# Attention, mixture of experts and feed-forward in one kernel: transposes moved a step, loads by head pair, weights placed earlier

## The chip, the cores and the metric
The kernel runs on one core of a Trainium2 chip. The metric is device time in microseconds (us) of one execution of the whole program; lower is better. Each version is run several times and the median counts.

The engines are named as in the profile: PE is TensorE (matmuls), PEld its weight loads, DVE is VectorE, ACT is ScalarE, POOL is GpSimd, and SP is the queue engine that issues most DMAs.

## The reference
The program computes three layers one after the other. B = 4 batches, H = 12 heads, S = 448 positions, D = 64; N = B*S = 1792 tokens with DM = 768 values; E = 8 experts with FF = 1024; the last layer has F2 = 2048.

```
scores = q @ k.T / sqrt(D) - log(S);  attn = sigmoid(scores);  x = attn @ v     # x: (N, DM)
logits = x @ w_gate;  e = argmax(logits);  g = softmax(logits)[e]
y = g * (relu(x @ w1[e]) @ w2[e])                                               # one expert per token
h = y @ w_in;  out = (h * sigmoid(h)) @ w_out
```

All operands are fp32, except that w_in and w_out arrive as 64-bit words that the kernel decodes.

## The kernel before
Every operand of the accurate matmuls is split into a high part rounded to fp32r and a low part, the difference; a product is three matmuls (high by high, low by high, high by low). The program's order on each engine is written out by hand: an engine runs its instructions in the order in which the code issues them, and waits where an operand isn't there. All DMAs but the gathers and scatters go through SP's queue, which is also in order.

Attention. A head pair (two heads) is handled in four half-steps k, each with 128 of the keys; there are 24 pairs, so k runs to G = 96 in a loop with step 2 (L616). One pass of the loop issues `scores(k)` and `scores(k+1)` (L212: score matmuls on half the rows of PE for each head, the sigmoid on ACT), then `av` of two half-steps earlier (L228: value matmuls in plain fp32), then DVE's splits of the next unit (two pairs, L180 to L204), then `evac` (L240: ACT copies a finished pair's output from PSUM), and then `background` (L604), which takes one `xform` from the list `xq`. `xform` (L246) is half a pair: two matmuls against the identity and the gate's weights (L258) transpose the output to token rows and give its part of the logits; DVE copies the rows (L260) and adds the logits (L265), and every second pair SP stores the rows to Xd (L268). After the last pair of a batch `route` (L270) works out experts, ranks and gate values in small DVE operations, some per half-step, and stores the gates to Gd (L365, rows of one value). After the third batch `choose` (L368) finds the expert with most tokens so far and SP loads its first-layer weights to stage1 (L390); in the last 12 half-steps they are split in half rows (L640 to L646, the subtractions half on DVE and half on POOL).

`load` (L167) fetches q, k and v of a unit of two pairs; two units are in flight.

Tiles of experts. Tile 0 belongs to the chosen expert. After the loop SP loads that expert's second-layer weights to stage2 (L746), `xtrans` (L673) transposes tile 0, the last `xform` and route run, `tables` (L418) lays out the other tiles in some 50 DVE operations, and `split2` (L692) splits stage2 on ACT, DVE and POOL. A tile (L802) is `l1` (L698), `relu`, `htrans` (L710), `l2` (L720) and `yout` (L736), which scales by the gate gathered from Gd (`gate`, L546). At an expert's last tile the next weights are split and loaded. The first expert's successor gets its stage2 in two parts during and after tile 1 (L827, L853).

Between the tiles `early` (L577) decodes six slices of w_in and w_out, one at a time; five are stored for later, one to the SBUF tile `sqp` and four to DRAM (Wd, L585), and `keep0` (L590) splits the sixth. The feed-forward layer begins with reloads from Wd on SP and POOL (L955), gathers of token rows (`xload`, L783), their transposes (L889, two PSUM buffers), and splits of the reloaded slices on ACT and DVE (`wlater`, L960). Then 112 steps of 18 plus 12 matmuls follow.

Of the kernel before, what the change touches and what calls it, by code (L numbers as in the profile page):

```python
# [26 lines left out]
E, FF = 8, 1024  # L27
# [30 lines left out]
def attn_moe_ffn(ctx: ExitStack, tc, qT, kT, v, wg, w1, w2, w_in, w_out, out):  # L58
# [19 lines left out]
    Wd = dp.tile([GROUPS[0], 128, 2, DM], F32, name="Wd")  # L78
# [46 lines left out]
    sqp = RX.pool("w10", 1).tile([128, DM], F32, name="w10")  # L125
# [14 lines left out]
    vp_ = LA.pool("a_v", 3)  # L140
    ld = LA.pool("a_load", 2)
# [9 lines left out]
    zero = c2.tile([128, YW], F32, name="zero")  # L151
    nc.vector.memset(zero, 0.0)
    xf = c2.tile([128, NP, 128 + E], F32, tag="xf", name="xf")
# [13 lines left out]
    def load(un, parts=(slice(0, 2),)):  # L167
        b, u = units[un]
        kf = ld.tile([128, 2, KP], F32, tag="kf", name=f"kf{un}")
        qf = ld.tile([128, 2, S], F32, tag="qf", name=f"qf{un}")  # L170
        vf = vp_.tile([128, 2, 4, 128], F32, tag="vf", name=f"vf{un}")
        for i, p in enumerate(parts):
            hs = slice(2 * u + p.start, 2 * u + p.stop)
            nc.sync.dma_start(out=kf[:, p], in_=kT[b, hs].rearrange("r p s -> p r s"))
            nc.sync.dma_start(out=qf[:, p], in_=qT[b, hs].rearrange("r p s -> p r s"))
            if i == 0:
                nc.sync.dma_start(out=vf, in_=v[b, :, 2 * u:2 * u + 2])
        loads[un] = kf, qf, vf

    def split_tiles(un):  # L180
        t = lambda n, w: sp_.tile([128, 2, w], F32R, tag=n, name=f"{n}{un}")
        ops[un] = t("kh", KP), t("kl", KP), t("qh", S), t("ql", S)

    def cast_k(un, p=slice(0, 2)):
        nc.vector.tensor_copy(out=ops[un][0][:, p], in_=loads[un][0][:, p])

    def sub_k(un, p=slice(0, 2)):
        kh, kl = ops[un][:2]
        nc.vector.tensor_sub(out=kl[:, p], in0=loads[un][0][:, p], in1=kh[:, p])

    def cast_q(un, p=slice(0, 2), copy=nc.vector.tensor_copy):
        copy(out=ops[un][2][:, p], in_=loads[un][1][:, p])

    def sub_q(un, p=slice(0, 2)):
        qh, ql = ops[un][2:]
        nc.vector.tensor_sub(out=ql[:, p], in0=loads[un][1][:, p], in1=qh[:, p])

    def first(p):
        cast_q(0, p, nc.scalar.copy)
        cast_k(0, p)  # L200
        sub_k(0, p)
        sub_q(0, p)

    SPLITS = (cast_k, cast_q, sub_k, sub_q)  # L204
# [7 lines left out]
    def scores(k):  # L212
        pr, g = divmod(k, NG)
        un, p = divmod(pr, 2)
        kh, kl, qh, ql = (t[:, p] for t in ops[un])
# [12 lines left out]
    def av(k):  # L228
        pr, g = divmod(k, NG)
        un, p = divmod(pr, 2)  # L230
        vf = loads[un][2]
        if g == 0:
            po[pr] = ps_o.tile([128, 512], F32, tag="o", name=f"o{pr}")
        a, n = gt.pop(k)
        for i in range(2):
            r = slice(64 * i, 64 * i + 64)
            nc.tensor.matmul(out=po[pr][r, 0:S], lhsT=vf[:, p, g, r], rhs=a[:, i if n == 2 else 0],  # L237
                             start=(g == 0), stop=(g == NG - 1))
# [31 lines left out]
    def route(b):  # L270
# [33 lines left out]
        nc.scalar.activation(out=sp, in_=z, func=AF.Sigmoid, bias=zero[:CP, 0:1])  # L304
        nc.scalar.activation(out=sn, in_=z, func=AF.Sigmoid, bias=zero[:CP, 0:1], scale=-1.0)
# [59 lines left out]
        nc.sync.dma_start(out=Gd[b * S:(b + 1) * S].rearrange("(c p) f -> p c f", p=CP), in_=gs.unsqueeze(2))  # L365
        yield "gs"

    def choose():  # L368
        yield 0
        pn = px_[1][:, 448:448 + E]  # L370
        nc.tensor.matmul(out=pn, lhsT=ones, rhs=run, start=True, stop=True)
        yield 0
        mx = rt.tile([128, 1], F32, tag="cmx", name="cmx")
        nc.vector.tensor_reduce(out=mx, in_=pn, axis=AX.X, op=ALU.max)
        yield 1
        cd = rt.tile([128, E], F32, tag="ccd", name="ccd")
# [12 lines left out]
        for i in range(KC):  # L389
            nc.sync.dma_start(out=stage1[:, i], in_=w1[bass.ds(er, 1), :, i].rearrange("a p f -> (a p) f"))  # L390
        yield 1
# [161 lines left out]
    load(0, (slice(0, 1), slice(1, 2)))  # L553
    load(1)
    split_tiles(0)
    first(slice(0, 1))
# [13 lines left out]
    PRE = [*range(1, 2 * GROUPS[0]), 0]  # L570
# [6 lines left out]
    def early():  # L577
        i = len(done)
        bt = c2.tile([128, DM], I32, tag="xf", name=f"btp{i}")
        sq = c2.tile([128, DM], F32, tag="sq", name=f"sqp{i}")  # L580
        for _ in decode(raws.pop(), sq, bt):
            pass
        f, o = divmod(PRE[i], 2)
        if PRE[i]:
            nc.sync.dma_start(out=sqp if (f, o) == (1, 0) else Wd[f, :, o], in_=sq)  # L585
# [4 lines left out]
    def keep0():  # L590
        wi = xr_p[1].tile([128, 2, DM], F32R, tag="xr", name="wi0")
        nc.scalar.copy(out=wi[:, 0], in_=done[-1])
        nc.vector.tensor_sub(out=wi[:, 1], in0=done[-1], in1=wi[:, 0])
# [10 lines left out]
    def background(k):  # L604
        for x in list(tasks):
            advance(x, RATE[x in fast])
        if xq and (k % 2 == 1 or k >= G - 4):
# [3 lines left out]
            if u == NU - 1 and pr % 2 == 1 and half == 1:  # L611
# [4 lines left out]
    for k in range(0, G + LAG + 2, 2):  # L616
        un, r = divmod(k, UG)
        if k < G:
            if r == (0 if un else 4) and un + 2 < len(units):
                load(un + 2)  # L620
            scores(k)
            scores(k + 1)
        if LAG <= k < G + LAG:
            av(k - LAG)
            av(k - LAG + 1)
        o = r - 2 * (un == 0)
        if k < G and un + 1 < len(units) and 0 <= o < len(SPLITS):
            if o == 0:
                split_tiles(un + 1)
            SPLITS[o](un + 1)  # L630
            SPLITS[o + 1](un + 1)
        if k == 0:
            first(slice(1, 2))
        if k >= LAG and (k - LAG) % NG == NG - 2:
            pr = (k - LAG) // NG
            evac(pr)
            xq += [(pr, 0), (pr, 1)]
        for j in (k, k + 1):
            background(j)
            if G - UG <= j < G - UG + 2 * KC:  # L640
                i, o = divmod(j - (G - UG), 2)
                hs = slice(o * HB, o * HB + HB)
                cast = nc.scalar.copy if i >= 4 else nc.vector.tensor_copy
                eng = nc.gpsimd if o else nc.vector
                cast(out=w1h[:, i, hs], in_=stage1[:, i, hs])
                eng.tensor_sub(out=w1l[:, i, hs], in0=stage1[:, i, hs], in1=w1h[:, i, hs])  # L646
# [12 lines left out]
    stage2 = wp2.tile([128, FC, DM], F32, name="stage2")  # L659
# [84 lines left out]
    er = reg(es_i[0:1, 0:1], (SP,), E - 1)  # L744
    for f in range(FC):
        nc.sync.dma_start(out=stage2[:, f], in_=w2[bass.ds(er, 1), :, f].rearrange("a p f -> (a p) f"))  # L746
    xhl = xtrans(0, cur[0])
    for x in xq:
        xform(*x)
# [52 lines left out]
    for t in range(TMAX):  # L802
# [6 lines left out]
        if t > 0:  # L809
# [16 lines left out]
            if t == 1:  # L826
                nc.sync.dma_start(out=stage2[:, 0:SA], in_=wsrc(w2, ne1, 0, SA))  # L827
            if len(done) == len(PRE) and not wi0:
# [23 lines left out]
        if t == 1:  # L852
            nc.sync.dma_start(out=stage2[:, SA:], in_=wsrc(w2, ne1, SA, FC))  # L853
# [8 lines left out]
    R0.close()  # L862
    M1.close()
# [79 lines left out]
    src = {(0, 1): dc.tile([128, DM], F32, tag="sq0", name="sqw")}  # L943
    for f in range(1, GROUPS[0]):
        w = wtile(0, f)
        wt[0, f] = w[:, 0], w[:, 1]
        r = dc.tile([128, 2, DM], F32, tag=f"raw{f % 2}", name=f"wd{f}")
        src[f, 0], src[f, 1] = sqp if f == 1 else r[:, 0], r[:, 1]
    later = sorted(src, key=lambda x: (x[0] + FLAG * x[1], x[1]))
    for i, (f, o) in enumerate(later):  # L950
        if i == 2:
            xts1 = xload(1)
        if i:
            eng = nc.sync if i < 2 else nc.gpsimd
            eng.dma_start(out=src[f, o], in_=Wd[f, :, o])  # L955
# [148 lines left out]
```

## Time and profile before

| | us |
|---|---|
| median of 3 runs | 1097.03 (1094.67 to 1097.07) |
| profiled execution | 1096.06 |
| its span | 1094.0 |
| PE busy | 1032.5 |
| DVE busy | 580.5 |
| ACT busy | 424.6 |
| POOL busy | 115.5 |

The span is the time between the first and the last record of the execution; what lies outside it belongs to start and end. The profile places attention at 0 to about 206 us, the tiles up to about 588 us, and the feed-forward layer behind that. "PEclk" and "granted clock" are the share of full speed at which PE ran (1.00 is 2.4 GHz, 0.50 is 1.2 GHz). A wait is written as the waiting instruction, an arrow, and the instruction that released it.

### The profile page before, as it was taken

How to read it: one execution, taken by the hardware profiler on the slowest of the kernel's cores; microseconds unless marked ns; L12 is line 12 of the kernel's file. 1: busy time of each engine (PE TensorE's matmuls, PEld its weight loads, DVE VectorE, ACT ScalarE, POOL GpSimd, SP SyncE). 2: the span in 40 equal slices, each digit the busy share in tenths (PEclk: the TensorE clock that was granted, in tenths of full speed). 3: DMA queues.
4: the chain of work that ended last, by engine and by line, in shares of the span. 5: the costliest groups of instructions: out<-in, count | busy, mean ns of one | idle time of the engine just before them, and what ended most of it. 6: DMA issues, size and time to landing. Idle time of an engine off the chain costs nothing. (4 is left out here: it accounts for less than half of the span.)

```text
span 1094.0 us, 16957 instructions
## 1 busy us (share of the span) xinstructions
PE 1032.5 (94%) x6418; PEld 901.3 (82%) x6418; DVE 580.5 (53%) x1167; ACT 424.6 (39%) x714; POOL 115.5 (11%) x106
## 2 busy tenths in 40 slices
PE   7999999888999999999997899999999999999996
PEld 4444444567987888888886899999999999999996
DVE  4234355583599218571712566476477455557443
ACT  5454444432487227462612455333233222223110
POOL 1000000331122202121112110000000000000022
PEclk9999999989999999999999899999999999999998
DMA  6444646449599317772624765564445544455572
GB/s 222 125 126 127 166 122 163 117 147 278 172 365 344 143 44 269 279 253 95 216 103 143 274 222 198 190 241 151 174 173 186 204 160 144 173 202 206 198 289 117
DMA packets 49150, 205.75 MB, mean 188 GB/s; under 512 B 7968, under 2 KB 16416, under 8 KB 45088
## 3 DMA queue, kind: packets, MB, share of 16 engines
q1 hardware_dynamic: 44288, 184.09, 48.5%
q0 software_dynamic: 4768, 20.47, 5.4%
q8 instruction: 52, 0.85, 0.3%
q14 instruction: 42, 0.34, 0.1%
HBM read 170.30 MB, written 33.84 MB: 187 GB/s over the span
## 5 line engine op out<-in xcount | busy, mean ns | idle before, releaser
L993 ACT ACTIVATE sg<-fh 128x256 f32<-128x256 f32 x112 | 42.9, 383 | 230.1 <-PE fh L991 218.1
L991 PE MATMUL fh<-rxh,w 128*128 128x256 f32 x462 | 130.5, 282 | 0.0
L990 PE MATMUL fh<-rxl,w 128*128 128x256 f32 x462 | 130.4, 282 | 0.0
L989 PE MATMUL fh<-rxh,w 128*128 128x256 f32 x462 | 130.2, 282 | 0.0
L1026 PE MATMUL fy<-w,gh 128*128 128x384 f32 x364 | 122.5, 337 | 0.4 <-DVE acc L1039 0.4
L1027 PE MATMUL fy<-w,gh 128*128 128x384 f32 x364 | 121.9, 335 | 0.0
L1028 PE MATMUL fy<-w,gl 128*128 128x384 f32 x364 | 121.8, 335 | 0.0
L224 ACT ACTIVATE a<-s,bias 128x896 f32<-128x896 f32 x96 | 82.7, 910 | 94.9 <-PE s L221 94.7
L994 DVE TENSOR_TENSOR sg<-sg,fh 128x256 f32<-128x256 f32 x112 | 47.0, 420 | 132.2 <-ACT sg L993 132.2
L728 PE MATMUL y<-w2h,hl 128*128 128x384 f32 x304 | 103.8, 342 | 10.2 <-DVE hl L717 7.0
L726 PE MATMUL y<-w2h,hh 128*128 128x384 f32 x304 | 106.3, 350 | 0.7 <-ACT hh L716 0.7
L727 PE MATMUL y<-w2l,hh 128*128 128x384 f32 x304 | 103.2, 339 | 0.5 <-POOL w2l L696 0.4
L703 PE MATMUL h<-w1h,xl 128*128 128x512 f32 x228 | 90.5, 397 | 2.9 <-DVE xl L684 2.9
L701 PE MATMUL h<-w1h,xh 128*128 128x512 f32 x228 | 92.3, 405 | 0.9 <-ACT xh L683 0.9
L702 PE MATMUL h<-w1l,xh 128*128 128x512 f32 x228 | 90.2, 396 | 0.0
L991 PEld LDWEIGHTS fh<-rxh,w 128*128 128x128 f32 x462 | 88.1, 191 | 0.0
L990 PEld LDWEIGHTS fh<-rxl,w 128*128 128x128 f32 x462 | 87.8, 190 | 0.0
L989 PEld LDWEIGHTS fh<-rxh,w 128*128 128x128 f32 x462 | 87.7, 190 | 0.0
L717 DVE TENSOR_TENSOR hl<-x,hh 128x512 fp32r<-128x512 f32 x38 | 26.2, 688 | 113.0 <-ACT hh L716 108.7
L237 PE MATMUL o<-a,vf 128*64 128x448 f32 x384 | 82.5, 552 | 0.0
L260 DVE COPY xr<-x 112x256 f32<-112x256 f32 x48 | 20.3, 424 | 106.6 <-PE x L258 106.6
L998 DVE TENSOR_TENSOR gl<-sg,gh 128x256 fp32r<-128x256 f32 x112 | 47.8, 426 | 52.9 <-ACT gh L997 51.5
(220 smaller groups left out, 2202.0 us busy)
## 6 DMA issues: line engine op xcount, KB each, us to landing
rxh<-Td SPq DMA_DIRECT2D x35, 768.0 KB
rxl<-Td SPq DMA_DIRECT2D x35, 768.0 KB
stage<-w SPq DMA_DIRECT2D x14, 1536.0 KB
stage<-w SPq DMA_DIRECT2D x8, 1920.0 KB
raw<-w_in SPq DMA_DIRECT2D x13, 768.0 KB
raw<-w_out SPq DMA_DIRECT2D x13, 768.0 KB
stage<-w SPq DMA_DIRECT2D x8, 1152.0 KB
Yd<-ys SPq DMA_DIRECT2D x19, 384.5 KB
```

The source lines that it names most:

```text
L701: nc.tensor.matmul(out=ph, lhsT=xh[:, k], rhs=w1h[:, k, cs], start=(k == 0), stop=False)
L702: nc.tensor.matmul(out=ph, lhsT=xh[:, k], rhs=w1l[:, k, cs], start=False, stop=False)
L703: nc.tensor.matmul(out=ph, lhsT=xl[:, k], rhs=w1h[:, k, cs], start=False, stop=(k == KC - 1))
L726: nc.tensor.matmul(out=o, lhsT=hh[:, c], rhs=w2h[:, f, ys], start=(f == 0), stop=False)
L727: nc.tensor.matmul(out=o, lhsT=hh[:, c], rhs=w2l[:, f, ys], start=False, stop=False)
L728: nc.tensor.matmul(out=o, lhsT=hl[:, c], rhs=w2h[:, f, ys], start=False, stop=(f == FC - 1))
L989: nc.tensor.matmul(out=ph, lhsT=ih[:, k], rhs=xh[:, k], start=(k == 0), stop=False)
L990: nc.tensor.matmul(out=ph, lhsT=ih[:, k], rhs=xl[:, k], start=False, stop=False)
L991: nc.tensor.matmul(out=ph, lhsT=il[:, k], rhs=xh[:, k], start=False, stop=(k == KC - 1))
L1026: nc.tensor.matmul(out=o, lhsT=gh[:, c], rhs=w[1][:, 0, ys], start=(f == 0), stop=False)
L1027: nc.tensor.matmul(out=o, lhsT=gh[:, c], rhs=w[1][:, 1, ys], start=False, stop=False)
L1028: nc.tensor.matmul(out=o, lhsT=gl[:, c], rhs=w[1][:, 0, ys], start=False, stop=last)
```

## The change
The transposing matmuls of a pair are issued in the pass after its `evac`, all of the pair's together, between that pass's scores and values; `background` no longer issues them. Loads and splits go by single pairs (q first), loads three pairs ahead. After `choose`, SP also loads the chosen expert's second-layer weights to stage2, which has its own place; the load after the loop is gone. The splits of stage1 go by whole rows, casts in turn on DVE and ACT, subtractions on DVE. Gd is stored from ACT's queue. `sqp` has four places: five of the six decoded slices stay there, one is stored to Wd and reloaded; the order of slices changes, and `keep0` runs as soon as two are decoded. The first part of the successor's stage2 load moves from the middle to the end of tile 1. The last route is no longer begun twice.

```diff
-    Wd = dp.tile([GROUPS[0], 128, 2, DM], F32, name="Wd")
+    Wd = dp.tile([128, DM], F32, name="Wd")
...
-    sqp = RX.pool("w10", 1).tile([128, DM], F32, name="w10")
+    sqp = RX.pool("w10", 1).tile([128, 4, DM], F32, name="w10")
+    RS = Group("right")
+    stage2 = RS.pool("stage2", 1).tile([128, FC, DM], F32, name="stage2")
...
-    vp_ = LA.pool("a_v", 3)
-    ld = LA.pool("a_load", 2)
+    vp_ = LA.pool("a_v", 5)
+    ld = LA.pool("a_load", 3)
...
+    def load(pr):
+        b, p6 = divmod(pr, NP)
+        kf = ld.tile([128, KP], F32, tag="kf", name=f"kf{pr}")
+        qf = ld.tile([128, S], F32, tag="qf", name=f"qf{pr}")
+        vf = vp_.tile([128, 4, 128], F32, tag="vf", name=f"vf{pr}")
+        nc.sync.dma_start(out=qf, in_=qT[b, p6])
+        nc.sync.dma_start(out=kf, in_=kT[b, p6])
+        nc.sync.dma_start(out=vf, in_=v[b, :, p6])
+        loads[pr] = kf, qf, vf
...
+    def split_k(pr):
+        kh, kl = ops[pr][:2]
+        nc.vector.tensor_copy(out=kh, in_=src(pr, 0))
+        nc.vector.tensor_sub(out=kl, in0=src(pr, 0), in1=kh)
+
+    def split_q(pr, copy=nc.vector.tensor_copy):
+        qh, ql = ops[pr][2:]
+        copy(out=qh, in_=src(pr, 1))
+        nc.vector.tensor_sub(out=ql, in0=src(pr, 1), in1=qh)
...
-        nc.sync.dma_start(out=Gd[b * S:(b + 1) * S].rearrange("(c p) f -> p c f", p=CP), in_=gs.unsqueeze(2))
+        nc.scalar.dma_start(out=Gd[b * S:(b + 1) * S].rearrange("(c p) f -> p c f", p=CP), in_=gs.unsqueeze(2))
...
             nc.sync.dma_start(out=stage1[:, i], in_=w1[bass.ds(er, 1), :, i].rearrange("a p f -> (a p) f"))
+        for f in range(FC):
+            nc.sync.dma_start(out=stage2[:, f], in_=w2[bass.ds(er, 1), :, f].rearrange("a p f -> (a p) f"))
...
-    load(0, (slice(0, 1), slice(1, 2)))
-    load(1)
+    for pr in range(3):
+        load(pr)
     split_tiles(0)
-    first(slice(0, 1))
+    split_q(0, nc.scalar.copy)
+    split_k(0)
...
-    PRE = [*range(1, 2 * GROUPS[0]), 0]
+    PRE = [2 * GROUPS[0] - 1, *range(2 * GROUPS[0] - 1)]
+    SLOT = [3, 3, 0, 1, 2, 3]
...
-        sq = c2.tile([128, DM], F32, tag="sq", name=f"sqp{i}")
+        sq = sqp[:, SLOT[i]]
...
-        f, o = divmod(PRE[i], 2)
-        if PRE[i]:
-            nc.sync.dma_start(out=sqp if (f, o) == (1, 0) else Wd[f, :, o], in_=sq)
+        if i == 0:
+            nc.sync.dma_start(out=Wd, in_=sq)
...
-        if xq and (k % 2 == 1 or k >= G - 4):
+
+    def wsplit0(i):
+        (nc.scalar.copy if i % 2 else nc.vector.tensor_copy)(out=w1h[:, i], in_=stage1[:, i])
+        nc.vector.tensor_sub(out=w1l[:, i], in0=stage1[:, i], in1=w1h[:, i])
+
+    def xforms():
+        while xq:
             pr, half = xq.pop(0)
             xform(pr, half)
...
-    for k in range(0, G + LAG + 2, 2):
-        un, r = divmod(k, UG)
+    for k in range(0, G + LAG, 2):
         if k < G:
-            if r == (0 if un else 4) and un + 2 < len(units):
-                load(un + 2)
+            if k % NG == 0 and k // NG + 3 < G // NG:
+                load(k // NG + 3)
             scores(k)
             scores(k + 1)
+        xforms()
         if LAG <= k < G + LAG:
             av(k - LAG)
             av(k - LAG + 1)
...
+        pn = k // NG + 1
+        if pn < G // NG:
+            if k % NG == 0:
+                split_tiles(pn)
+                split_k(pn)
+            else:
+                split_q(pn)
...
+        if k >= G - UG:
+            wsplit0((k - G + UG) // 2)
...
-    er = reg(es_i[0:1, 0:1], (SP,), E - 1)
-    for f in range(FC):
-        nc.sync.dma_start(out=stage2[:, f], in_=w2[bass.ds(er, 1), :, f].rearrange("a p f -> (a p) f"))
     xhl = xtrans(0, cur[0])
-    for x in xq:
-        xform(*x)
+    xforms()
+    wsplit0(KC - 1)
...
-            if t == 1:
-                nc.sync.dma_start(out=stage2[:, 0:SA], in_=wsrc(w2, ne1, 0, SA))
-            if len(done) == len(PRE) and not wi0:
+            if len(done) >= 2 and not wi0:
                 keep0()
...
         if t == 1:
+            nc.sync.dma_start(out=stage2[:, 0:SA], in_=wsrc(w2, ne1, 0, SA))
             nc.sync.dma_start(out=stage2[:, SA:], in_=wsrc(w2, ne1, SA, FC))
...
+    wl = dc.tile([128, 2, DM], F32, tag="raw0", name="wl")[:, 0]
+    nc.sync.dma_start(out=wl, in_=Wd)
+    src = {divmod(PRE[i], 2): sqp[:, SLOT[i]] for i in range(2, len(PRE))} | {divmod(PRE[0], 2): wl}
...
-    for i, (f, o) in enumerate(later):
-        if i == 2:
-            xts1 = xload(1)
-        if i:
-            eng = nc.sync if i < 2 else nc.gpsimd
-            eng.dma_start(out=src[f, o], in_=Wd[f, :, o])
+    xts1 = xload(1)
```

## Rows read from the trace of the kernel before
**Rows 1.** The page's first part: busy time, share of the span, instructions of each engine.

```profile
PE 1032.5 (94%) x6418; PEld 901.3 (82%) x6418; DVE 580.5 (53%) x1167; ACT 424.6 (39%) x714; POOL 115.5 (11%) x106
```

**Rows 2.** Stretches: us; busy PE, PEld, DVE, ACT, POOL (instructions); granted clock; DMA share; GB/s.

```profile
16.00:206.00 190.00, 175.58 (x1040) 91.40 (x1038) 81.78 (x256) 90.25 (x118) 6.34 (x6) 1.00 0.48 131
...
225.00:231.00 6.00, 4.93 (x15) 4.33 (x16) 5.32 (x14) 2.26 (x4) 3.07 (x2) 0.50 0.00 0
...
270.00:273.00 3.00, 3.00 (x10) 2.56 (x11) 0.69 (x1) 0.58 (x1) 0.00 (x0) 0.55 0.89 302
...
598.00:606.00 8.00, 0.72 (x4) 0.73 (x5) 4.11 (x9) 4.24 (x8) 0.00 (x0) 0.65 0.96 395
606.00:611.00 5.00, 5.00 (x25) 5.00 (x24) 2.50 (x4) 1.39 (x3) 2.12 (x2) 0.54 0.66 202
```

**Rows 3.** Waits of the whole span: us in total, times, longest.

```profile
POOL gg L548 <- DMA Gd<-gs: 23.4, 1, 23.4
...
PE x L258 <- ACT ot L244: 14.5, 23, 0.6
...
ACT w2h L694 <- DMA stage<-w: 6.9, 1, 6.9
...
ACT w L965 <- DMA wd<-Wd: 4.4, 1, 4.4
...
PE x L713 <- ACT hs L707: 4.0, 1, 4.0
...
ACT ys L739 <- DMA gg<-Gd,gi: 3.7, 1, 3.7
...
PE h L703 <- DVE xl L684: 2.9, 2, 2.3
...
PE x L349 <- DVE pb L341: 2.5, 4, 1.3
```

**Rows 4.** Instructions in time, one head pair: start, us, what, idle before and releaser.

```profile
107.45 0.72 PE L258 MATMUL x<-xf,ot 128*112 128x136 f32 x4 [0.63 <-ACT ot L244]
108.10 0.47 PE L221 MATMUL s<-qh,kh 64*128 64x448 f32 x2
...
109.70 1.72 PE L237 MATMUL o<-a,vf 128*64 128x448 f32 x8
...
115.20 0.53 ACT L244 COPY ot<-o 128x448 f32<-128x448 f32 x1 [0.31 <-PE o L237]
...
115.79 0.72 PE L258 MATMUL x<-xf,ot 128*112 128x136 f32 x4 [0.63 <-ACT ot L244]
```

**Rows 5.** Instructions in time, PE near the end of attention.

```profile
200.44 1.18 PE L258 MATMUL x<-xf,ot 128*112 128x136 f32 x8 [0.63 <-ACT ot L244]
...
201.55 0.47 PE L221 MATMUL s<-qh,kh 64*128 64x448 f32 x2
```

**Rows 6.** Instructions in time, PE and its weight loads at the start.

```profile
10.03 1.73 PE L237 MATMUL o<-a,vf 128*64 128x448 f32 x8
...
11.68 0.19 PEld L221 LDWEIGHTS s<-qh,kh 64*128 64x128 f32 x2 [0.70 <-ACT a L224]
...
11.68 0.48 PE L221 MATMUL s<-qh,kh 64*128 64x448 f32 x2
```

**Rows 7.** Instructions in time, DVE: half of q's split, a copy of transposed rows.

```profile
9.71 0.63 DVE L196 TENSOR_TENSOR ql<-qf,qh 128x448 fp32r<-128x448 f32 x1
...
112.11 0.42 DVE L260 COPY xr<-x 112x256 f32<-112x256 f32 x1 [0.97 <-PE x L258]
```

**Rows 8.** SP's DMA issues late in attention, and a stretch's busy times as in rows 2.

```profile
172.60 3.16 SPq L390 DMA_DIRECT2D stage<-w  x6
...
175.00:180.00 5.00, 4.75 (x31) 2.66 (x31) 3.89 (x11) 1.72 (x3) 0.00 (x0) 1.00 1.02 399
```

**Rows 9.** SP's DMA issues between tile 0 and tile 1.

```profile
241.84 0.34 SPq L774 DMA_DIRECT2D stage<-w  x1
243.08 0.33 SPq L365 DMA_DIRECT2D Gd<-gs  x1
```

More of the change, by code (lines that the diff above doesn't have):

```diff
@@ L150, in attn_moe_ffn @@
     nc.scalar.activation(out=c2.tile([128, 1], F32, name="pre"), in_=bias, func=AF.Sigmoid)
-    zero = c2.tile([128, YW], F32, name="zero")
+    zero = sqp.rearrange("p n d -> p (n d)")[:, 0:YW]
     nc.vector.memset(zero, 0.0)
+    zb = c2.tile([128, 1], F32, name="zb")
+    nc.vector.memset(zb, 0.0)
     xf = c2.tile([128, NP, 128 + E], F32, tag="xf", name="xf")
@@ L165, in attn_moe_ffn @@
     ops = {}
[L167 to L204, printed above, removed]
+    def load(pr):
[7 more added lines that the diff above has]
+        loads[pr] = kf, qf, vf
@@ new lines, in split_tiles, with src @@
+    def split_tiles(pr):
+        t = lambda n, w: sp_.tile([128, w], F32R, tag=n, name=f"{n}{pr}")
+        ops[pr] = t("kh", KP), t("kl", KP), t("qh", S), t("ql", S)
+    def src(pr, i):
+        return loads[pr][i]
+    def split_k(pr):
[6 more added lines that the diff above has]
+        nc.vector.tensor_sub(out=ql, in0=src(pr, 1), in1=qh)
@@ L214, in scores @@
         un, p = divmod(pr, 2)
-        kh, kl, qh, ql = (t[:, p] for t in ops[un])
+        kh, kl, qh, ql = ops[pr]
         ps = ps_s.tile([128, 2, 512], F32, tag="s", name=f"s{k}")
@@ L230, in av @@
         un, p = divmod(pr, 2)
-        vf = loads[un][2]
+        vf = loads[pr][2]
         if g == 0:
@@ L236, in av @@
             r = slice(64 * i, 64 * i + 64)
-            nc.tensor.matmul(out=po[pr][r, 0:S], lhsT=vf[:, p, g, r], rhs=a[:, i if n == 2 else 0],
+            nc.tensor.matmul(out=po[pr][r, 0:S], lhsT=vf[:, g, r], rhs=a[:, i if n == 2 else 0],
                              start=(g == 0), stop=(g == NG - 1))
@@ L303, in route @@
         sn = tl("sn", [CP, NC, E])
-        nc.scalar.activation(out=sp, in_=z, func=AF.Sigmoid, bias=zero[:CP, 0:1])
-        nc.scalar.activation(out=sn, in_=z, func=AF.Sigmoid, bias=zero[:CP, 0:1], scale=-1.0)
+        nc.scalar.activation(out=sp, in_=z, func=AF.Sigmoid, bias=zb[:CP, 0:1])
+        nc.scalar.activation(out=sn, in_=z, func=AF.Sigmoid, bias=zb[:CP, 0:1], scale=-1.0)
         yield 0
@@ L591, in keep0 @@
         wi = xr_p[1].tile([128, 2, DM], F32R, tag="xr", name="wi0")
-        nc.scalar.copy(out=wi[:, 0], in_=done[-1])
-        nc.vector.tensor_sub(out=wi[:, 1], in0=done[-1], in1=wi[:, 0])
+        nc.scalar.copy(out=wi[:, 0], in_=done[1])
+        nc.vector.tensor_sub(out=wi[:, 1], in0=done[1], in1=wi[:, 0])
         wi0.append(wi)
@@ L610, in background @@
             b, u = units[pr // 2]
-            if u == NU - 1 and pr % 2 == 1 and half == 1:
+            if u == NU - 1 and pr % 2 == 1 and half == 1 and b < B - 1:
                 tasks.append(route(b))
@@ L625, in attn_moe_ffn @@
             av(k - LAG + 1)
[L626 to L633, printed above, removed]
+        pn = k // NG + 1
[5 more added lines that the diff above has]
+                split_q(pn)
         if k >= LAG and (k - LAG) % NG == NG - 2:
@@ L637, in attn_moe_ffn @@
             xq += [(pr, 0), (pr, 1)]
+        if k >= G - UG:
+            wsplit0((k - G + UG) // 2)
         for j in (k, k + 1):
             background(j)
[L640 to L646, printed above, removed]
             if cur is None and j >= G - 8 and not tasks:
@@ L658, in attn_moe_ffn @@
     wp2 = M2.pool("m_w2", 1)
-    stage2 = wp2.tile([128, FC, DM], F32, name="stage2")
     w2h = wp2.tile([128, FC, DM], F32R, name="w2h")
@@ L862, in attn_moe_ffn @@
     R0.close()
+    RS.close()
     M1.close()
@@ L942, in attn_moe_ffn @@
     wt[0, 0] = wi0[0], w00[:, 1]
-    src = {(0, 1): dc.tile([128, DM], F32, tag="sq0", name="sqw")}
+    wl = dc.tile([128, 2, DM], F32, tag="raw0", name="wl")[:, 0]
+    nc.sync.dma_start(out=wl, in_=Wd)
+    src = {divmod(PRE[i], 2): sqp[:, SLOT[i]] for i in range(2, len(PRE))} | {divmod(PRE[0], 2): wl}
     for f in range(1, GROUPS[0]):
@@ L946, in attn_moe_ffn @@
         wt[0, f] = w[:, 0], w[:, 1]
-        r = dc.tile([128, 2, DM], F32, tag=f"raw{f % 2}", name=f"wd{f}")
-        src[f, 0], src[f, 1] = sqp if f == 1 else r[:, 0], r[:, 1]
     later = sorted(src, key=lambda x: (x[0] + FLAG * x[1], x[1]))
-    for i, (f, o) in enumerate(later):
-        if i == 2:
-            xts1 = xload(1)
-        if i:
-            eng = nc.sync if i < 2 else nc.gpsimd
-            eng.dma_start(out=src[f, o], in_=Wd[f, :, o])
+    xts1 = xload(1)
     for xhl in xtr(0, xts):
```

## Prediction
> **What bounds the kernel now.** I read the engine totals first, then busy time by stretch, then the list of waits, and only then the order of single instructions where a wait was long. TensorE (PE) is busy 94% of the span [rows 1]: 1094.0 - 1032.5 = 61.5 us idle are all that a better order can win, besides time lost at the lower clock. By stretch [rows 2] the idle time lies in four places. Attention (16 to 206 us) has 14.4 us of it spread evenly. From 225 to 231 PE is busy but the granted clock is 0.50, the 1.2 GHz level. From 270 to 273 the clock is 0.55, after a wait of 4.0 us [rows 3]. From 598 to 606 PE works 0.72 us of 8, and to 611 the clock is 0.54. The waits name the causes [rows 3]: in attention the transposing matmuls L258 wait 14.5 us in 23 waits for ScalarE's copy L244; at 266 the transposes L713 wait 4.0 us for ScalarE, whose queue stands 3.7 us behind the gathered gate, and a gather of that gate waited 23.4 us for the store of Gd; at 598 ScalarE's cast L965 waits for decoded weights read back from Wd, and the transposes L889 stand behind it. No other engine is the bound: in attention VectorE (DVE) is busy 82 us and ScalarE 90 us of 190 [rows 2].
>
> **Attention: transposes one step later.** One head pair takes 115.79 - 107.45 = 8.34 us [rows 4]. PE's order is transposes, scores, values, transposes, scores, values; L258 is issued right after the values, and the copy L244 (0.53 us) can start only when these end, so PE waits 0.63 us. After the change eight L258 stand behind the next scores. These take 109.70 - 108.10 = 1.60 us, the copy needs 0.53 and a start some 0.3 us after the values: it is hidden with 0.8 us to spare. 23 waits of 0.63 us go: -14.5 us. Also, two groups of four L258 cost 0.65 us each (107.45 to 108.10), while eight in a row cost 201.55 - 200.44 = 1.11 us [rows 5]: 0.19 us a pair, -4 us over 23 pairs. New is scores directly behind values. At the start of the trace they are already so once: values from 10.03 for 1.73 us, scores at 11.68, just before their recorded end [rows 6], so this edge costs about what the old one did. Its bounds are -0.1 and +0.2 us a time, 47 times; I take +0.01, nearest to that row: +0.5 us. Attention: -18 us.
>
> What is late next? In the step with the transposes DVE does two copies of 0.42 us and two additions to the logits, about 0.16 us each (an estimate from the copy's length and size), then the q split of the next pair: a cast, put at 0.4 us (an estimate, two thirds of the subtraction of the same tile), and the 0.63 us subtraction [rows 7]. The second copy can start when the second four L258 end; from there copy, addition, cast and subtraction are 1.6 us. PE meanwhile runs values for 1.73 us [rows 6], and the low half of q is needed only by the third of six groups of score matmuls, a quarter of 1.6 us later. So it fits with about 0.5 us, and I cost it at 0; without that cover each pair would lose what the split is late.
>
> **Loads and splits by pair.** The same bytes move. DVE runs two instructions of half the width where it ran one; even if a half cost as much as a whole, that is some 2 us more in a pair's 8 us (two casts and two subtractions like those of [rows 7], doubled) on an engine that is busy 82 of 190 us: 0. At the start q comes before k and both halves of q precede k on DVE: the first scores are at most 0.6 us later, but ScalarE no longer casts pair 1's q between sigmoids: 0, bounds -1 and +1 us. Loads run three pairs ahead and are split one pair ahead, so two pairs, some 15 us, cover a late landing.
>
> **Second-layer weights staged in attention.** SP issues the first six weight loads from 172.60 [rows 8]; now eight more (3 MB) follow them, and the last pair's q, k and v come behind 6.3 MB. At the 399 GB/s of 175 to 180 us that is 16 us, at 300 GB/s, my estimate with other traffic beside it, 21. The last pair's split is due 10 half-steps later, 10 x (8.34 - 0.82) / 4 = 19 us, its scores 26 us later. I take 0; bound +4 us. Yd's blank rows and Xd's stores queue behind them too, but these are read only in the tiles.
>
> **From attention to tiles.** What goes: the 2.3 us in which L703 waits for DVE [rows 3], since first-layer transposes now precede the last L258 and the last split is one; ScalarE's 6.9 us wait for the second weights, behind which DVE held the routing tables. So the table chain begins earlier, by 2 us in my estimate (a third of the 6.9), the 2.5 us in which L349 waits for L341 [rows 3] shrinks, and if PE idles less before 225 the clock need not fall: 6 us at 0.50 cost 3. Together 2.3 + 2.5 + 3 = 7.8 at best. Against it: DVE now subtracts whole rows that GpSimd shared, and the rank matmuls now reach PE before the route on DVE is done; I estimate that wait at up to the 2.3 us of L703 that goes. I take -4.5 us, bounds -8 and 0.
>
> **Gd's store on ScalarE's queue.** It is issued at 243.08, 1.2 us after a 3 MB load on the same queue [rows 9], and its gather starts only when the 23.4 us wait ends. At 399 GB/s [rows 8] that load alone holds it for 3.1 / 0.399 = 8 us. Off that queue it starts at once and should be done as much earlier; then the gate is there when tile 1 ends, and 4.0 us idle and 3 x 0.45 = 1.3 us of clock [rows 2] go. The stage2 load behind it in line moves to the end of tile 1; it is read only at the next expert. ScalarE's queue now waits for DVE's last gate operation, four times, with sigmoids or a square behind it: under 1 us each, 0 to +3, I take +1. Sum: -5 + 1 = -4 us.
>
> The Trainium skill ("DMA: Bandwidth & Descriptors", Rules for kernel authors) says that spreading transfers over issuing engines doesn't help, since all run on the same 16 DMA engines. By that rule the store would land no earlier and this term would be 0; the 23.4 us in the row contain both the queue and the store itself and cannot tell which.
>
> **Decoded weights in SBUF.** Four of five stores and three of four reloads go. L965's casts no longer wait, so the third group of L889 waits only for two ScalarE copies and one DVE subtraction: about 1.2 us instead of 7.3 [rows 2]: -6 us. The clock then has no reason to fall; 606 to 611 at 0.54 returns 5 x 0.46 = 2.3 us. The one remaining reload is cast last, a step later. -8.3 us, bounds -5 and -9.5. Keeping the first expanded weight at tile 2 instead of 5 moves one cast and one subtraction to another tile, where PE has as much to do: 0.
>
> **Sum.** -18 - 4.5 - 4 - 8.3 = -34.8 us. The profiled execution took 1096.06 us, 2.06 outside its span; 1096.06 - 34.8 = 1061.3, and its time lies 1.0 us under the median: **1062 us**.
>
> **Rivals.**
> (a) Gd stays late on any queue, and the stall at 266 remains: +5, 1067 us. For it: the store writes rows of single values; against it: 3 MB stood ahead of it.
> (b) The change doesn't shorten attention as it says: DVE's q split, behind copies that now wait for all eight L258, becomes what scores wait for and eats most of the gain, say 0.6 us a pair: 1062 + 14 = 1076 us. For it: my margin is 0.5 us. Against: DVE is under half busy in attention.
> (c) The last loads behind 6.3 MB, or weights behind them, are late: +4, 1066 us.
> (d) Slower: scores right behind values cost a bare weight load each time, 47 times. The weight loads stand idle 0.70 us there [rows 6]; were all of it exposed, that is 33 us, the whole gain within 2 us. From 34.8 / 47 = 0.74 us an edge on the change is slower; at 0.85 us, with a start of 0.15 us on top, the time is 1062 + 40 = 1102 us. Against it: PE's matmuls in the same rows follow without a gap.
>
> **How the numbers follow.** Forecast 0.70, (a) 0.12, (b) 0.09, (c) 0.05, (d) 0.04. The forecast's own terms span 1062 - 9 (edges -0.1, -8, -9.5) to about 1072; (a) and (c) lie inside, (b) reaches 1076. So 1053 to 1076 leaves out about 2 in 10. A measurement of this kernel tells 0.3% (3.3 us) from no change; only (d) and worse cases of (b) get there: faster 0.93, same 0.03, slower 0.04.
>
> **What would show it.** Right, step by step: a pair takes 7.5 to 7.6 us, L258 has no wait for L244; no idle at PE before the second tile's L713; L889's wait under 2 us and no 0.5 clock at either place; the chosen expert's L694 starts without a DMA wait. Wrong: scores waiting for a split in attention, gathers of Gd still waiting 20 us, a new wait of DVE for kf late in attention, or a pair still over 8 us.

## The result and the profile after

The changed kernel takes 1065.91 us (median of 4 runs, 1065.14 to 1068.31) against 1097.05 us for the kernel before, run beside it (4 runs, 1094.67 to 1099.21): ratio 0.972, 95% interval 0.9695 to 0.9746. The forecast was 1062, the range 1053 to 1076. The profiled execution took 1065.88 us, its span is 1064.1.

The page's first part, after; it answers to [rows 1]:

```profile
PE 1022.5 (96%) x6418; PEld 902.6 (85%) x6418; DVE 585.1 (55%) x1204; ACT 425.6 (40%) x712; POOL 109.0 (10%) x97
```

PE's idle time fell from 61.5 us to 41.6. The other 10 us of the gain are in PE's busy time. Of these 7.4 lie in attention (186.6 us before, 179.2 after, up to the last values matmul). The granted clock did not rise there (1.00 before, 0.98 after), so they come of the new order of the matmuls. The rest, 1.8 and 1.3 us, lies in the two parts behind, where the clock rose from 0.90 to 0.94 and from 0.95 to 1.00 and a matmul counts shorter.

To see where the time went I cut both spans at four events on PE, all read from the order of its instructions (us from the span's start):

| event | before | after | part's change |
|---|---|---|---|
| last values matmul of attention ends | 206.38 | 190.77 | -15.6 |
| first transposes for tile 1 (before L678, after L673) | 239.12 | 218.16 | -5.35 |
| first transposes for tile 3, in tile 2 | 273.74 | 249.25 | -3.5 |
| end of the span | 1094.0 | 1064.1 | -5.4 |

The last values matmuls, before and after (start and us; their sum is the first event):

```profile
203.15 3.23 PE L237 MATMUL o<-a,vf 128*64 128x448 f32 x16
```

```profile
187.54 3.23 PE L230 MATMUL o<-a,vf 128*64 128x448 f32 x16
```

Stretches of the changed kernel, with the columns of [rows 2], which they answer to: attention, its end, the transition, the wait in tile 2, and three pieces of the feed-forward layer's start:

```profile
16.00:190.80 174.80, 168.47 (x1040) 93.89 (x1036) 89.80 (x298) 92.17 (x120) 3.20 (x2) 0.98 0.60 166
...
175.00:180.00 5.00, 0.07 (x2) 0.10 (x2) 4.66 (x13) 0.00 (x0) 1.04 (x1) 0.74 0.35 128
180.00:185.00 5.00, 5.00 (x22) 2.60 (x22) 3.41 (x4) 2.02 (x2) 2.15 (x2) 0.58 0.62 172
...
210.00:215.00 5.00, 4.75 (x24) 4.43 (x23) 3.69 (x7) 3.53 (x5) 4.31 (x4) 0.85 0.50 141
245.00:250.00 5.00, 3.26 (x20) 2.52 (x19) 0.69 (x1) 1.35 (x3) 0.00 (x0) 1.00 0.93 244
566.00:570.00 4.00, 3.85 (x20) 3.85 (x21) 2.34 (x4) 1.32 (x2) 2.67 (x3) 0.57 0.77 243
571.00:576.00 5.00, 2.50 (x22) 2.26 (x20) 3.75 (x9) 3.36 (x7) 0.00 (x0) 1.00 1.00 402
576.00:580.50 4.50, 4.04 (x21) 4.04 (x22) 3.37 (x5) 2.12 (x4) 2.38 (x2) 0.62 0.45 152
```

Two of the old holes are smaller (the transition's clock is 0.85 where it was 0.50; in tile 2 PE loses 1.74 us, now for gathered rows, where it lost 4.0 for ScalarE), the one at the feed-forward start is halved, and one is new: from 175 to 180 us, inside attention, PE does 0.07 us of work, and then runs at 0.58, near the 1.2 GHz level.

The waits of the whole span, with the columns of [rows 3]:

```profile
POOL gg L543 <- DVE btp L103: 22.5, 1, 22.5
...
DVE kh L190 <- DMA kf<-kT: 10.8, 2, 9.0
...
PE s L214 <- DVE qh L195: 6.3, 1, 6.3
...
PE ft L881 <- DVE fxl L884: 4.0, 2, 3.0
...
PE t L673 <- DMA gx<-Xd,gi: 1.7, 1, 1.7
...
PE h L698 <- DVE xl L679: 0.6, 1, 0.6
```

The 14.5 us in 23 waits of the transposing matmuls (now L251) for the copy (now L237) have no row any more, nor have the waits of w2h for stage2 and of the casts for Wd. New are the waits for late k: 9.0 us on DVE and 6.3 us on PE. The gather of the gate still waits 22.5 us (put down here to a DVE instruction, long done: the store of Gd lands last).

One pair of the changed kernel, as [rows 4] (start, us, what):

```profile
95.89 0.53 ACT L237 COPY ot<-o 128x448 f32<-128x448 f32 x1 [0.31 <-PE o L230]
...
97.29 1.09 PE L251 MATMUL x<-xf,ot 128*112 128x136 f32 x8
...
98.31 1.72 PE L230 MATMUL o<-a,vf 128*64 128x448 f32 x8
...
103.02 0.47 PE L214 MATMUL s<-qh,kh 64*128 64x448 f32 x2
...
104.53 1.09 PE L251 MATMUL x<-xf,ot 128*112 128x136 f32 x8
```

The copy ends 0.87 us before L251 starts, so nothing waits, and a pair takes 104.53 - 97.29 = 7.24 us, against 8.34.

### The profile page after: what moved, and what is told of

Same layout as the page of the kernel before. It is cut to its first block, busy times and chain, and to the rows that moved or that the text cites. A ratio compares the mean times of both kernels' runs of the same rounds, so it can differ in the third digit from the quotient of the medians.

```text
span 1064.1 us, 17019 instructions
## 1 busy us (share of the span) xinstructions
PE 1022.5 (96%) x6418; PEld 902.6 (85%) x6418; DVE 585.1 (55%) x1204; ACT 425.6 (40%) x712; POOL 109.0 (10%) x97
## 5 line engine op out<-in xcount | busy, mean ns | idle before, releaser
L984 ACT CAST gh<-sg 128x256 fp32r<-128x256 f32 x112 | 45.5, 407 | 67.7 <-DVE sg L981 67.7
```

## Experiments

All but e5 and e10 start from the changed kernel with the loads of the first experiment. Ratios are to the kernel before, run beside each on the same chip, with 95% intervals; where two runs were on different chips, the ratios are compared.

**1. The late loads: e1_loads_first, and again as e11_loads_first_again.** The changed kernel's end of attention, first SP's issues, then DVE and PE:

```profile
149.69 3.29 SPq L383 DMA_DIRECT2D stage<-w  x6
153.16 9.51 SPq L385 DMA_DIRECT2D stage<-w  x8
163.36 0.34 SPq L176 DMA_DIRECT2D qf<-qT  x1
164.28 0.34 SPq L177 DMA_DIRECT2D kf<-kT  x1
```

```profile
175.21 0.43 DVE L190 CAST kh<-kf 128x512 fp32r<-128x512 f32 x1 [8.97 <-DMA kf<-kT]
...
179.93 0.74 PE L214 MATMUL s<-qh,kh 64*128 64x448 f32 x2 [6.29 <-DVE qh L195]
```

The last pair's k is issued 14.6 us after the first weight load, because the eight stage2 issues ahead of it take SP 9.5 us, and DVE can cast it only 10.9 us later still. Behind that cast DVE, which works in order, has a cast and a subtraction for w1, two copies and the q split, and PE waits for the cast of q.

```diff
         for i in range(KC):
             nc.sync.dma_start(out=stage1[:, i], ...)
+        yield 0
+        yield 0
         for f in range(FC):
             nc.sync.dma_start(out=stage2[:, f], ...)
```

> The eight stage2 loads are issued two half-steps later, behind the last pair's q, k and v. Theory 1 (order on SP: the last pairs' loads are late because the weights stand ahead of them): TensorE's two waits of 6.3 and 5.3 us for the splits qh and kh near 160 and 180 us go, and the clock of 0.58 to 0.74 behind them with them; about 11.6 us and 2 us of clock, so 1053 us against 1066 of the changed kernel. Rival (bytes: the DMA engines are full in this stretch, so something stays late whatever the order): the waits move to other loads or to the chosen expert's second-layer casts, and the time stays at 1062 to 1066 us.

Measured: 1059.03 us (1055.67 to 1064.7, 4 runs), ratio 0.9659 [0.9614, 0.9703]. SP's issues in e1:

```profile
155.59 0.68 SPq L176 DMA_DIRECT2D qf<-qT  x1
156.32 0.57 SPq L177 DMA_DIRECT2D kf<-kT  x1
...
158.25 13.59 SPq L387 DMA_DIRECT2D stage<-w  x8
```

Its last values matmuls:

```profile
178.49 3.23 PE L230 MATMUL o<-a,vf 128*64 128x448 f32 x16
```

Values end at 181.71 instead of 190.77: 9.1 us, the wait of 6.3 and the clock behind it. No other load is late, so it was the order on SP and not the bytes that made k late: theory 1 holds. One store is late now: behind the loop DVE waits 6.2 us, until 182.04, for rows that go to Xd behind the eight issues (4.7 us in e11). What of this reaches PE isn't separated; its next wait, L700 for DVE, is 1.9 us in e1 and 0.4 in e11. I had expected 11.6 us of waits; 5.3 of them were the wait for the first scores of the kernel, which the same row sums up and which stays.

The four times spread over 9 us, so I ran the same kernel again.

> The same kernel as e1_loads_first, beside e9 and e10 on the same chip, because its four times spread over 9 us (1055.7 to 1064.7) where others spread over 2 to 4. If the spread was chance, the median lies at 1057 to 1060 us with a spread like that of the others; if this order of loads makes the time uncertain, times over 1062 us come again.

Measured: 1056.52 us (1053.89 to 1059.52, 5 runs), ratio 0.9658 [0.9641, 0.9675]. The median agrees, the interval is now clear of the changed kernel's. The two profiled executions of this one program, 1061.33 and 1053.89 us, show where it spreads. Stretches of the first, then of the second:

```profile
240.00:245.00 5.00, 2.75 (x16) 2.23 (x15) 0.91 (x3) 1.79 (x4) 0.00 (x0) 0.94 0.86 297
245.00:250.00 5.00, 5.00 (x25) 4.91 (x24) 2.79 (x7) 1.86 (x3) 1.75 (x2) 0.72 0.96 394
...
565.00:570.00 5.00, 5.00 (x30) 5.00 (x30) 2.20 (x4) 1.95 (x4) 1.65 (x1) 0.64 0.96 346
```

```profile
240.00:245.00 5.00, 5.00 (x34) 4.96 (x33) 3.47 (x8) 3.05 (x5) 0.59 (x1) 1.00 1.01 368
245.00:250.00 5.00, 5.00 (x30) 4.86 (x28) 3.20 (x5) 0.54 (x2) 1.69 (x2) 1.00 0.94 374
...
565.00:570.00 5.00, 3.94 (x30) 3.94 (x31) 4.38 (x9) 3.32 (x7) 2.48 (x2) 1.00 0.75 279
```

In tile 2 the first waits 2.2 us for rows of gx and the second 0.5, and the clock falls in the first alone. At the feed-forward start the three waits of the transposes sum to 5.2 us in both (1.78 + 1.01 + 2.40 and 1.40 + 1.01 + 2.79), and again only the first loses clock, 0.64 from 565 to 570. From tile 1's transposes to tile 3's the first takes 32.5 us and the second 29.9, from there to the end 816.4 and 812.4. Of these 4.0 us, 1.6 are lost right behind tile 3's transposes (the 0.72 from 245 to 250) and 2.4 at the feed-forward start. Differences of 3 us in one stage of one profile therefore decide nothing here; I go by the runs' intervals.

**2. The transposes: e2_transposes_at_once.** On top of e1:

```diff
             scores(k + 1)
-        xforms()
...
             xq += [(pr, 0), (pr, 1)]
+            if k < G:
+                xforms()
```

> As e1_loads_first, but each pair's transposing matmuls stand right behind its values again, all eight in a row; loads and splits by pair stay. Theory 1 (the gain of a pair is the wait for the copy that now lies behind scores): transposes wait for ScalarE's copy again, 0.6 to 0.7 us or more in each of 23 pairs, and the cost is 15 to 24 us over e1_loads_first; a pair takes 7.9 to 8.3 us. Rival (the gain comes from loads and splits by pair, fewer interruptions on ScalarE and DVE): a pair stays at 7.3 to 7.5 us and the time within 5 us of e1_loads_first.

Measured: 1079.49 us (4 runs), ratio 0.9855 [0.9829, 0.988], 20.5 us over e1. Two of its pairs:

```profile
97.43 1.18 PE L251 MATMUL x<-xf,ot 128*112 128x136 f32 x8 [0.63 <-ACT ot L237]
...
105.55 1.18 PE L251 MATMUL x<-xf,ot 128*112 128x136 f32 x8 [0.63 <-ACT ot L237]
```

The wait is back in every pair, and a pair takes 8.12 us. That separates the gain: from 8.34 to 8.12 by putting eight transposing matmuls in a row (0.22 us), from 8.12 to 7.24 by their place (0.88). Of the 0.88, 0.63 is the wait; 0.09 is that eight L251 behind scores take 98.31 - 97.29 = 1.02 us and not 1.11 as behind the wait. Most of the rest is the step out of scores: the last score matmuls start 0.20 us before transposes and 0.30 us before values.

**3. Gd's queue and the moved load: e3_gd_sp, e4_w2_mid_tile1, e8_gd_sp_w2_mid.** e3 and e4 undo one edit each, e8 both. The moved load is the first part of stage2, 1920 KB (the expectations say 3 MB). The 3 MB load ahead of the store [rows 9] is another, of first-layer weights; the change doesn't move it, and it goes out ahead of the store in every kernel here (220.91 and 222.14 in the changed kernel).

```diff
-        nc.scalar.dma_start(out=Gd[...], in_=gs.unsqueeze(2))
+        nc.sync.dma_start(out=Gd[...], in_=gs.unsqueeze(2))
...
+            if t == 1:
+                nc.sync.dma_start(out=stage2[:, 0:SA], in_=wsrc(w2, ne1, 0, SA))
             if len(done) >= 2 and not wi0:
...
         if t == 1:
-            nc.sync.dma_start(out=stage2[:, 0:SA], in_=wsrc(w2, ne1, 0, SA))
             nc.sync.dma_start(out=stage2[:, SA:], in_=wsrc(w2, ne1, SA, FC))
```

> As e1_loads_first, but Gd is stored from SP's queue again, while the 3 MB load stays behind tile 1. Queue theory (the prediction's term: the queue keeps the store late): Gd lands later, the gate of tile 1 with it, and the time is about 4 to 5 us over e1_loads_first. Rival (the store is slow by itself on any queue, about 17 us from issue to landing, and what helped is that the 3 MB load no longer lies beside the gathers behind it): 17 to 18 us from issue to landing again, and the time within 1 us of e1_loads_first.

> As e1_loads_first, but the 3 MB stage2 load is issued in the middle of tile 1 again, while Gd's store stays on ScalarE's queue. Queue theory: Gd is ahead of it on another queue, so nothing changes: within 1 us of e1_loads_first. Rival (that load slows the store's last packets and the gathers of Gd and gx): the gathers take 6 to 7 us instead of 3, TensorE's wait ahead of tile 2 grows from 1.7 to about 4 to 5 us, and the time is 3 to 4 us over e1_loads_first.

> As e1_loads_first, but both edits around Gd are undone together, as before the change: Gd is stored from SP's queue, and the 3 MB load is issued in the middle of tile 1. e3 and e4 undid one each: the queue gave 17.0 against 18.0 us from issue to landing and no loss of time, the position of the load a wait of 3.6 us ahead of tile 2 and the 1.2 GHz clock behind it. If the two are independent, this kernel stands where e4_w2_mid_tile1 does, about 3 us over e1_loads_first (ratio to the kernel before 0.967 to 0.971). Rival (queue and load act together: Gd's store stands behind the load's eight descriptors on the same queue): Gd lands later than in e4_w2_mid_tile1, and the cost is 5 us or more.

Measured: e3 1056.91 us, 0.9636 [0.961, 0.9663]; e4 1061.9 us, 0.969 [0.9667, 0.9713]; e8 1061.5 us, 0.9682 [0.9658, 0.9706]. The store's own row, in e3 (SP's queue) and in the changed kernel (ScalarE's):

```profile
L358 SPq DMA_DIRECT2D Gd<-gs x1: 328/328/328, 216.0 to 216.0; - x1
...
DMA to landing us min/median/max: 17.0/17.0/17.0
```

```profile
L358 ACTq DMA_DIRECT2D Gd<-gs x1: 311/311/311, 222.1 to 222.1; - x1
...
DMA to landing us min/median/max: 17.2/17.2/17.2
```

e1 has 18.0 on ScalarE's queue, e8 18.1 on SP's, and before the change the gather that waits for it started at 261.49, 18.4 us after the issue [rows 9]. In e3 the 3 MB load stands 1.1 us ahead of the store on the same queue, in the changed kernel on the other, and the store takes 17.0 and 17.2 us: its queue is worth nothing. This is the Trainium skill's rule that the prediction set against its own term ("DMA: Bandwidth & Descriptors", Rules for kernel authors: spreading DMAs over issuing engines for bandwidth doesn't help), and these two rows agree with it. That the store is slow by itself is only half shown. The stores of the first two batches, as large and with no weight load beside them, landed after 8.6 to 12.1 us in these profiles; so the 3 MB beside the last one, on whichever queue, may cost it the rest, and no run takes that load away.

What did help is the moved load's position, about 0.3% (0.969 and 0.9682 against 0.9658; e4's interval is clear of e3's and just overlaps e11's, e8's overlaps both). The profiles say it more clearly: from tile 1's transposes to tile 3's it takes 34.9 us in e4 and 34.3 in e8, as before the change (34.6), and 28.4 to 32.5 in the nine other experiments. In e4 the gather of the gate and the first instruction that reads it:

```profile
233.84 1.02 POOL L545 DMA_INDIRECT gg<-Gd,gi  x1 [24.46 <-DMA Gd<-gs]
...
239.13 0.90 ACT L736 ACTIVATE ys<-y,gg 128x768 f32<-128x768 f32 x1 [4.80 <-DMA gg<-Gd,gi]
```

Stretches of e4 (first fence) and e3 behind the store:

```profile
233.00:237.00 4.00, 4.00 (x19) 3.06 (x17) 3.50 (x5) 0.95 (x1) 2.58 (x2) 1.00 0.91 373
237.00:240.00 3.00, 0.22 (x1) 0.00 (x0) 0.00 (x0) 0.87 (x1) 1.00 (x1) 0.95 0.91 326
240.00:245.00 5.00, 4.15 (x12) 3.49 (x13) 0.69 (x1) 1.21 (x3) 0.00 (x0) 0.50 0.94 289
```

```profile
233.00:237.00 4.00, 4.00 (x18) 3.21 (x18) 1.76 (x2) 1.45 (x2) 3.01 (x3) 1.00 0.51 169
```

With 373 GB/s beside it the gathered gate is read 5.3 us after the gather starts; ScalarE waits 4.8 us for it, PE then 3.6 (L710 for hs), and runs at 0.50 afterwards. With 169 GB/s beside it ScalarE waits 0.3 us. The two edits are independent, as e8 = e4 says; in e8 the store is issued ahead of the moved load, which is one issue (215.36 and 221.49 on SP), so the order that its rival speaks of doesn't arise.

**4. Is the staging in attention worth anything? e5_w2_after_loop.** The changed kernel, with stage2 loaded behind the loop as before:

```diff
-        for f in range(FC):
-            nc.sync.dma_start(out=stage2[:, f], ...)
         yield 1
...
+    er = reg(es_i[0:1, 0:1], (SP,), E - 1)
+    for f in range(FC):
+        nc.sync.dma_start(out=stage2[:, f], ...)
     xhl = xtrans(0, cur[0])
```

> The changed kernel, but the chosen expert's second-layer weights are loaded behind the attention loop again, as before the change; everything else stays. If staging these 3 MB in attention is what made the last pairs' loads late: attention ends 9 us earlier, as in e1_loads_first (values done near 182 us instead of 190.8), but ScalarE's cast of these weights waits for them again, 4 to 7 us, as before; the time is 1057 to 1062 us, above e1_loads_first by what the transition loses (0 to 4 us). Rival (staging in attention pays: TensorE stood 7 us behind this load before): the transition takes over 5 us longer than in e1_loads_first, 1063 us or more. The prediction's bounds for this part were 0 for the staging and -8 to 0 for the transition.

Measured: 1057.66 us (5 runs), ratio 0.9649 [0.9624, 0.9674], as e1. The wait of 4 to 7 us for these weights, which I expected back, did not come: w2h has no wait for a DMA. The reason is in SP's order. Before the change (first fence) and in e5:

```profile
197.22 13.33 SPq L268 DMA_DIRECT2D Xd<-xr  x2
211.41 3.82 SPq L746 DMA_DIRECT2D stage<-w  x6
```

```profile
159.91 13.45 SPq L261 DMA_DIRECT2D Xd<-xr  x2
174.16 5.12 SPq L739 DMA_DIRECT2D stage<-w  x8
186.54 0.33 SPq L261 DMA_DIRECT2D Xd<-xr  x1
```

Before, the load stood behind the store of the last transposed rows and went out at 211.41. With the last transposes moved behind the loop that store comes after the load, which goes out at 174.16 from the same place in the code. So the second-layer weights are early without being staged; staging them in attention added nothing and cost 7 to 8 us (ratios 0.9649 to 0.9659 against 0.972). What made them early isn't separated: besides the order, stage2 has its own place since the change, and in e5 too. Before, it is laid out behind the loop in the space that attention's buffers leave (L655 to L659), so that load had to wait for the end of attention, whatever stood ahead of it on SP.

**5. The feed-forward start: e9_decode_dram, e6_splits_late.** e9 puts the stores to Wd and the reloads back on top of e1; e6 delays casts of later weights.

```diff
-        if i == 0:
-            nc.sync.dma_start(out=Wd, in_=sq)
+        f, o = divmod(PRE[i], 2)
+        if (f, o) not in ((0, 0), (1, 0)):
+            nc.sync.dma_start(out=Wd[f, :, o], in_=sq)
...
+        if (f, o) != (1, 0):
+            eng = nc.sync if i < 2 else nc.gpsimd
+            eng.dma_start(out=src[f, o], in_=Wd[f, :, o])
```

> As e1_loads_first, but the decoded weights go through DRAM again, as before the change: four of them are stored to Wd and loaded again ahead of the last network, and only (1, 0) stays in SBUF; the order in which they are decoded stays that of the change. Theory (the reloads make ScalarE's cast wait, and the third group of transposes with it): the wait for DMA at L952 and a wait of TensorE of 5 to 7 us near 560 to 570 us come back with the 1.2 GHz clock behind them, 4 to 6 us over e1_loads_first, 1062 to 1065 us. Rival (what moved this stage is the clock alone, or the reloads hide behind the token transposes): within 1.5 us of e1_loads_first.

Measured: 1063.39 us (5 runs), ratio 0.9717 [0.9704, 0.9731], beside e11's 1056.52, 0.9658: 6.9 us, a little more than I expected. From tile 3's transposes to the end it takes 820.0 us, as before the change (820.3), and 812.4 to 816.4 in the ten other experiments. Its wait and its third group of transposes, then those of e11:

```profile
ACT w L960 <- DMA wd<-Wd: 3.8, 1, 3.8
```

```profile
572.00 1.11 PE L884 MATMUL ft<-ident,stage 128*128 128x128 f32 x4 [6.84 <-DVE fxl L887]
```

```profile
566.06 0.66 PE L883 MATMUL ft<-ident,stage 128*128 128x128 f32 x4 [2.79 <-DVE fxl L886]
```

The reloads cost PE 6.84 - 2.79 = 4.1 us of waiting; the rest is clock (0.50 from 570 to 575 in e9).

```diff
-            wlater(2)
+            wlater(0 if s == 0 else 4)
```

> As e1_loads_first, but in the first step of the last network no weights of later steps are cast, so that ScalarE and VectorE have only the tokens' casts there; four are made in each step after it. Theory (the third group of L881 waits 2.4 to 3.0 us because casts and subtractions of later weights stand ahead of its own on ScalarE and VectorE): that wait falls to about 1 us, and the time is 1.5 to 2.5 us under e1_loads_first (1054 to 1057 us). Rival (it waits for its loads or for the two VectorE passes of its own): the wait stays over 2 us and the time within 1 us of e1_loads_first, or later steps wait for the casts put off and it is slower.

Measured: 1058.38 us (5 runs), ratio 0.9653 [0.9631, 0.9674], as e1 and e11. The wait that I aimed at fell, from 2.40 and 2.79 in the two profiles of e1's kernel to 1.71, and one for a delayed cast took part of its place:

```profile
568.36 0.66 PE L883 MATMUL ft<-ident,stage 128*128 128x128 f32 x4 [1.71 <-DVE fxl L886]
...
569.84 0.52 PE L980 MATMUL fh<-fxh,w 128*128 128x256 f32 x1 [0.49 <-DVE w L955]
```

What is left, 0.2 to 0.6 us, is below what the runs can tell. That the delayed casts caused 0.7 to 1.1 us of the wait is shown in one profile; the 1.71 that stay and a gain are not.

**6. Together: e7_all and e10_best.** e7 adds to e6 a later gather of tile 1's gate; e10 is e7 with the loads of e5.

```diff
-            gg = gate(t, gi)
+            if t != 1:
+                gg = gate(t, gi)
...
             nn = prep(t + 2) if t + 2 < TMAX else None
+            if t == 1:
+                gg = gate(t, gi)
```

> As e6_splits_late, and the gate of tile 1 is gathered behind the rows of tile 3 instead of ahead of them, so that GpSimd's wait for Gd no longer stands ahead of the gather of gx. Theory (TensorE's wait ahead of tile 2 is the late gx, and Gd's own 17 to 18 us are then covered by the rest of tile 1): no wait of TensorE between tiles 1 and 2, 2 to 4 us under e6_splits_late, 1051 to 1054 us. Rival (the gate itself is needed by then): ScalarE's L736 waits for gg, TensorE waits as long for a later tile, and nothing is gained.

> The loads of e5_w2_after_loop with the two edits of e7_all: second-layer weights loaded behind the attention loop, no casts of later weights in the first step of the last network, the gate of tile 1 gathered behind the rows of tile 3. If the three are independent: e5 (1057.7) less what e7 gained over e6 and e1 (2 to 3 us), 1054 to 1056 us. Rival (each only moves the same slack, and what is left is set by the clock): 1056 to 1058 us, as e5 and e7.

Measured: e7 1056.05 us, 0.9637 [0.9615, 0.9659]; e10 1054.94 us (1053.98 to 1055.54, 5 runs), 0.9639 [0.9626, 0.9652]. In e7 no wait for gx is left, but PE waits 1.3 us for ScalarE (L710 for hs), which stands behind the gate: part of the rival's path. Neither is clear of e1, e3 or e5. e10 is the version that I would keep: its interval is clear of both the kernel before and the changed kernel (0.972 [0.9695, 0.9746]), and its five times lie within 1.6 us. Its profile has PE busy for 1017.5 us, 97% of the span.

## Why the prediction was right, and which of its terms were not

The time and its sign came out right, 3.9 us above the forecast, but partly by luck, because errors cancel: one term was 7 us too small, and one that stood at 0 cost 7 to 9. Of its own signs, L251 indeed waits for no copy and a pair takes even less than 7.5 us, but two of its signs of being wrong came as well: the gather of Gd still waited over 20 us, and DVE waited for kf late in attention. The bounds were also added up wrongly: the lower terms make 9.9 us and not 9, and about 1072 is what the edges and the start alone give; with the upper bounds of the other terms it would be near 1086. The measured time is inside either way.

- **Attention, -18 forecast; the transposes give -24.7** (206.38 to 181.71 in e1). The mechanism is right: e2 brings the wait back. The merging was worth 0.22 us a pair for 0.19 forecast. The mis-sized term is the edges, "about what the old one did": a pair shrank by 1.10 us, not 0.82, so 0.28 x 23 = 6.4 us were missing. I had priced scores behind values but not transposes behind scores, where the group starts sooner and takes 1.02 us, not 1.11. Rival (d), a bare weight load at each edge, is refuted by the same rows; rival (b) too: with the loads in order PE waits for no split of q.
- **Weights staged, 0 forecast with a bound of +4; it cost 9.1 us of attention** (e1), 7 to 8 in the runs (e1, e5, e11). Rival (c), at 0.05, is what happened, and larger. The step that failed is "I take 0": my own 21 us of loads exceeded the 19 us until the split was due, I let the 26 us until the scores stand in for it, and I left out that DVE does its work in order, so that a late k holds the q split and the copies behind it. The trace has k cast 25.5 us after the first weight issue.
- **Transition, -4.5 forecast, -5.35 measured** in the changed kernel, -2.5 to -5.1 in the profiles of the others. The 2.3 us wait shrank to 0.6 and the clock fell less, as forecast. The wait for w2h went as well, but it goes without the staging too (e5).
- **Gd, -4 forecast, -3.5 measured, by another mechanism.** The step that failed is "off that queue it starts at once and should be done as much earlier": it took 17.2 us again, and rival (a) was right about the store. Yet the stall shrank from 4.0 to 1.7, because the first stage2 load (1920 KB), which my account moved at no gain, no longer ran beside the gathers behind the store (e4, e8). The +1 us for ScalarE's queue isn't seen: e3, without it, is not clear of e1 and e11.
- **Feed-forward start, -8.3 forecast, -5.4 in the profile (from tile 3's transposes to the end), -6.9 by e9.** Waits for Wd are gone as forecast (of the six slices `sqp` keeps four, not five as said under the change: one is split at once, one goes over Wd). The third group's wait is 2.96 us and not 1.2: I counted only its own copies and subtraction, but two casts and two subtractions of later weights stand ahead of them on ScalarE and DVE (e6, which delays them, has 1.71). The clock still fell behind the waits that are left, to 0.57 and 0.62; in e11 it stayed at 1.00.

What stays open: why the clock falls in one execution and not in another after waits of about the same length, whether the later gather of the gate gains anything, what holds SP between the issues of the weight loads, and how much of the last Gd store's 17 us the 3 MB load beside it makes.

## What to carry to other kernels

A load that is moved ahead of a deadline pushes back everything issued behind it on its queue, by the time its issues hold the queue as well as by its bytes: compare the landing with the first in-order consumer's due time, and count what stands behind that consumer. Before staging data earlier, look why the old load was late: here it stood behind a store and waited for attention's space, and other parts of the same change took both away. Where two edits are made for one wait, undo each alone; here the one argued for did nothing and the other did the work.

## What the runs showed of the hardware

- The last of the four stores of Gd, 1.8 KB in single values, took 14.9 to 19.3 us from issue to landing in the twelve profiles since the change, on SP's queue and on ScalarE's, each time beside a 3 MB load. With the 1920 KB load beside it too it took 19.2 (e4) and 18.1 (e8). The first two stores, of the same size, took 8.6 to 12.1.
- Eight issues of a 3 MB load, 0.33 us each in the changed kernel, spread over 9.5 us on SP's queue there, 13.6 in e1 and 5.1 in e5.
- Eight transposing matmuls of 136 columns took 1.02 us behind scores and 1.11 behind a wait.
- One program differed by 7.4 us between two executions. Of these 2.4 lie at the feed-forward start, where the waits sum to the same 5.2 us and the granted clock is 0.64 in one and 1.00 in the other.
